# Decode attention with a key/value cache: values summed two key columns per matmul, fewer columns scored on TensorE, short last chunks, a column-shaped output side, and a weight loaded in pieces

## The chip, the cores and the metric

The kernel runs on one core of a Trainium2 chip. The metric is the device time of one execution in microseconds (us). A profile is one further execution under the hardware profiler.

Engine names: PE is TensorE (PEld its weight loads), DVE is VectorE, ACT is ScalarE, SP is the engine that issues the DMAs here. A "DMA engine" is one of the 16 whose busy share the profile's page gives beside these; that is another thing than the engines just named, and most of this study is about one of the 16.

## The reference, cut to what matters

```python
# one query token; H = 32 heads, Sk = 32768 cached keys, Dh = 192, D = 640, Dff = 1536, all bf16
q = (layernorm(x) @ wq).reshape(1, 1, H, Dh).transpose(0, 2, 1, 3)
scores = einsum("bhqd,bhkd->bhqk", q, k_cache) * Dh ** -0.5
o = einsum("bhqk,bhkd->bhqd", softmax(scores), v_cache)
h = x + o.transpose(0, 2, 1, 3).reshape(1, 1, H * Dh) @ wo
out = h + relu(layernorm(h) @ w1) @ w2
```

Each key and value is used once, so the work is reading 805 MB of K and V (2 x 32 x 32768 x 192 x 2 bytes) and about 20 MB of weights.

## The kernel before

A chunk is 4096 keys of one head: 128 partitions with J = 32 key columns of 192 elements each. There are 8 chunks a head, 256 in all. Ten of the 32 columns are scored on TensorE (transpose, copy, matmul), 22 on VectorE, one instruction a column.

```python
J = 32; CH = P * J; NC = Sk // CH; JP = 10; JD = J - JP
kpool = ...tile_pool(name="kpool", bufs=5)          # 5 K tiles, 5 V tiles
vpool = ...tile_pool(name="vpool", bufs=5)

def load_kv(g):                                     # 12288 contiguous bytes a partition
    kt = kpool.tile([P, J * Dh], bf16, name="kt")
    nc.sync.dma_start(out=kt[:], in_=k_hd[h, c * CH:(c + 1) * CH, :].rearrange("(p j) d -> p (j d)", p=P))
    ... # vt the same

def scores_dve(g, mid=None):
    for j in range(JD):
        if j == 4 and mid is not None: mid()        # once a head: the previous head's denominator
        st = scp.tile([P, Dh], bf16, name="st")
        nc.vector.scalar_tensor_tensor(out=st[:], in0=kt[:, j * Dh:(j + 1) * Dh], scalar=1.0, in1=qb[:],
                                       op0=A.mult, op1=A.mult, accum_out=sc[:, j:j + 1])

def pv(g):                                          # o[1, 192] += p_column.T @ V_column, 32 times
    for jj in range(J):
        ...
        nc.tensor.matmul(o[:], lhsT=p, rhs=vt[:, j * Dh:(j + 1) * Dh], start=..., stop=...)

# main loop, cut:
    load_kv(g)
    ... # wo, wq loads
    if c == 0 and h == H // 2:
        nc.sync.dma_start(out=w1_sb[:], in_=B_w1.rearrange("(c p) n -> p c n", p=P))
    if c == 0 and h == H // 2 + 1:
        nc.sync.dma_start(out=w2_sb[:], in_=B_w2.rearrange("(c p) n -> p c n", p=P))
    transposes(g); pv(g - 1); scores_pe(g); scores_dve(g); ...; exp_dve(g, sc)
pv(G - 1); den_mm(H - 1); den_rec(H - 1); o_scale(H - 1); o_turn(...); project(...)
... # layernorm, w1, relu; then the w2 product as rows: 12 x (512 + 128) output columns on one partition
```

The softmax here doesn't subtract the row's maximum and nothing guards it: scores larger than these inputs give would overflow.

Of the kernel before, what the change touches and what calls it, by code (L numbers as in the profile page):

```python
# [13 lines left out]
def kernel(  # L14
# [26 lines left out]
    J = 32  # L41
    CH = P * J
    NC = Sk // CH
    G = H * NC
    JP = 10
    JD = J - JP
    NB = JP * Dh // P
    QG = 4
    assert Sk % CH == 0 and 2 * Dh == 3 * P and JP % 2 == 0 and H % QG == 0 and H % 2 == 0
# [44 lines left out]
    def load_kv(g):  # L94
        h, c = divmod(g, NC)
        kt = kpool.tile([P, J * Dh], bf16, name="kt")
        nc.sync.dma_start(out=kt[:], in_=k_hd[h, c * CH:(c + 1) * CH, :].rearrange("(p j) d -> p (j d)", p=P))
        vt = vpool.tile([P, J * Dh], bf16, name="vt")
        nc.sync.dma_start(out=vt[:], in_=v_hd[h, c * CH:(c + 1) * CH, :].rearrange("(p j) d -> p (j d)", p=P))
        kt_t[g], vt_t[g] = kt, vt  # L100
# [10 lines left out]
    ones_col = const.tile([P, 1], f32)  # L111
# [8 lines left out]
    dsums = const.tile([P, H, 2 * NC], f32)  # L120
    w1_sb = const.tile([P, DT, Dff], bf16)
    w2_sb = const.tile([P, FT, D], bf16)
    o_pair = [const.tile([1, 2 * Dh], f32, name=f"o_pair{i}") for i in range(2)]
# [25 lines left out]
    with tc.manual_schedule():  # L149
# [37 lines left out]
        def transposes(g):  # L187
            kt = kt_t[g]
            kT = tsb.tile([P, NB, P], bf16, name="kT")
            for b0 in range(0, NB, 8):  # L190
                nb = min(8, NB - b0)
                tp = tps.tile([P, 8, P], bf16, name="tp")
                for b in range(nb):
                    off = JD * Dh + (b0 + b) * P
                    nc.tensor.transpose(out=tp[:, b, :], in_=kt[:, off:off + P], identity=ident_b[:])  # L195
                nc.scalar.copy(out=kT[:, b0:b0 + nb, :], in_=tp[:, 0:nb, :])  # L196
            kT_t[g] = kT

        def scores_pe(g):
            kT = kT_t.pop(g)  # L200
            h, c = divmod(g, NC)
            qm = qm_t[h]
            sp = sps.tile([P, JP], f32, name="sp")
            for i in range(JP // 2):
                nc.tensor.matmul(sp[:, 2 * i:2 * i + 2], lhsT=kT[:, 3 * i + 1, :], rhs=qm[:, 1:3],  # L205
                                 start=True, stop=False, skip_group_check=True)
                nc.tensor.matmul(sp[:, 2 * i:2 * i + 1], lhsT=kT[:, 3 * i, :], rhs=qm[:, 0:1],  # L207
                                 start=False, stop=False, skip_group_check=True)
                nc.tensor.matmul(sp[:, 2 * i + 1:2 * i + 2], lhsT=kT[:, 3 * i + 2, :], rhs=qm[:, 3:4],  # L209
                                 start=False, stop=True, skip_group_check=True)  # L210
            pB = pcp.tile([P, JP], bf16, name="pB")
            nc.scalar.activation(out=pB[:], in_=sp[:], func=F.Exp, scale=SCALE,  # L212
                                 accum_out=dsums[:, h, 2 * c + 1:2 * c + 2])
            pB_t[g] = pB

        def scores_dve(g, mid=None):
            kt = kt_t.pop(g)
            h, c = divmod(g, NC)
            qb = qb_t[h]
            sc = scp.tile([P, JD], f32, name="sc")  # L220
            for j in range(JD):
                if j == 4 and mid is not None:
                    mid()
                st = scp.tile([P, Dh], bf16, name="st")
                nc.vector.scalar_tensor_tensor(out=st[:], in0=kt[:, j * Dh:(j + 1) * Dh], scalar=1.0, in1=qb[:],  # L225
                                               op0=A.mult, op1=A.mult, accum_out=sc[:, j:j + 1])
            return sc

        def exp_dve(g, sc):
            h, c = divmod(g, NC)  # L230
            pA = pcp.tile([P, JD], bf16, name="pA")
            nc.scalar.activation(out=pA[:], in_=sc[:], func=F.Exp, scale=SCALE,  # L232
                                 accum_out=dsums[:, h, 2 * c:2 * c + 1])
            pA_t[g] = pA

        def pv(g):
            h, c = divmod(g, NC)
            vt, pA, pB = vt_t.pop(g), pA_t.pop(g), pB_t.pop(g)
            if c == 0:
                o_t[h] = ops.tile([1, Dh], f32, name="o_ps")  # L240
            o = o_t[h]
            for jj in range(J):
                j = jj + JD if jj < JP else jj - JP
                p = pA[:, j:j + 1] if j < JD else pB[:, j - JD:j - JD + 1]
                nc.tensor.matmul(o[:], lhsT=p, rhs=vt[:, j * Dh:(j + 1) * Dh],  # L245
                                 start=(c == 0 and jj == 0), stop=(c == NC - 1 and jj == J - 1))
# [3 lines left out]
        def den_mm(h):  # L250
            d = mm_bank([1, 2 * NC], f32, "den")
# [3 lines left out]
        def den_rec(h):  # L255
            d = den_t.pop(h)
            s = small.tile([1, 2], f32, tag="rec", name="rec")
# [4 lines left out]
        def o_scale(h):  # L262
            s = den_t.pop(h)
            o = o_t.pop(h)
            nc.scalar.activation(out=o_pair[(h // 2) % 2][0:1, (h % 2) * Dh:(h % 2 + 1) * Dh], in_=o[:],  # L265
                                 func=F.Copy, scale=s[0:1, 1:2])
# [3 lines left out]
        def o_turn(pr):  # L270
            ps = mm_bank([P, 3], f32, "oT_ps")
            for b in range(3):
                nc.tensor.transpose(out=ps[:, b:b + 1], in_=o_pair[pr % 2][0:1, b * P:(b + 1) * P],  # L273
                                    identity=ident_f[0:1, 0:1])
# [15 lines left out]
        for g in range(G):  # L290
            h, c = divmod(g, NC)
# [6 lines left out]
            if c == 0 and h == H // 2:  # L298
                nc.sync.dma_start(out=w1_sb[:], in_=B_w1.rearrange("(c p) n -> p c n", p=P))
            if c == 0 and h == H // 2 + 1:  # L300
# [20 lines left out]
        pv(G - 1)  # L321
        den_mm(H - 1)
        den_rec(H - 1)
        o_scale(H - 1)
# [7 lines left out]
        y_a = ops.tile([1, 512], f32, tag="o_ps", name="y_a")  # L332
        y_b = ops.tile([1, P], f32, tag="o_ps", name="y_b")
        for c in range(DT):
            y = y_a[0:1, c * P:(c + 1) * P] if c < 4 else y_b[0:1, :]
            nc.tensor.matmul(y, lhsT=h_col[:, c:c + 1], rhs=ident_f[:], start=(c == 0 or c == 4),  # L336
                             stop=False, skip_group_check=True)
        h1ps = mm_bank([P, FT], f32, "h1ps")
# [6 lines left out]
        for f in range(FT):  # L345
            nc.tensor.matmul(y_a[:], lhsT=h1T[:, f:f + 1], rhs=w2_sb[:, f, 0:512],  # L346
                             start=False, stop=(f == FT - 1), skip_group_check=True)
            nc.tensor.matmul(y_b[:], lhsT=h1T[:, f:f + 1], rhs=w2_sb[:, f, 512:D],  # L348
                             start=False, stop=(f == FT - 1), skip_group_check=True)
        y_row = small.tile([1, D], bf16, tag="y_row", name="y_row")  # L350
        nc.scalar.copy(out=y_row[0:1, 0:512], in_=y_a[:])  # L351
        nc.vector.tensor_copy(out=y_row[0:1, 512:D], in_=y_b[:])
        nc.sync.dma_start(out=out.rearrange("b s d -> (b s) d"), in_=y_row[:])
# [30 lines left out]
```

## Time and profile before

| | before |
|---|---|
| time, median of runs | 2060.8 us (2060.41 to 2061.72) |
| span of the profiled run | 2060.4 us |
| last V tile landed | 2039.3 us |
| from there to the end | 21.1 us |

The first fence is from the page of the kernel before: busy time of each engine; what the 16 DMA engines moved in each of 40 slices of the span; and the DMA queues (packets, MB, share of 16 engines' span). Queue 1 moves 825.00 MB, which is K, V and the weights; the page gives queues 8 and 14 the kind "instruction". Queue 8 is read as TensorE's: its packets (16384 bytes each) are 130 where there are 16643 matmuls, one for every 128 matmuls.

```profile
PE 1405.5 (68%) x16643; PEld 1193.5 (58%) x16643; DVE 1603.1 (78%) x11352; ACT 651.6 (32%) x1719; POOL 0.7 (0%) x6
...
GB/s 395 423 421 420 423 421 423 407 422 420 423 422 357 423 418 423 416 346 425 382 420 344 418 423 421 423 423 393 425 421 422 414 350 423 420 423 417 397 412 77
...
q1 hardware_dynamic: 87596, 825.00, 96.5%
q8 instruction: 130, 2.13, 0.4%
q14 instruction: 118, 0.97, 0.1%
```

The reader sees queue 1 busy for 96.5% of what 16 engines could be, and yet slices at 344 to 393 GB/s among slices at 423. The second fence is the same page's groups for the scoring line (count, then busy us and mean ns of one).

```profile
L225 DVE SCALAR_TENSOR_TENSOR st<-kt,qb 128x192 bf16<-128x192 bf16 x5632 | 1589.7, 350 | 306.7 <-DMA kt<-in_A_k_cache_dram 294.7
...
L225 DVE DVE_READ_ACCUMULATOR st<-kt,qb 128x1 f32 x5632 | 442.4, 79 | 0.1
```

Each column is two rows in the trace on VectorE, the product and the accumulator read. The third fence is from the waits of the kernel before (total us, times, longest).

```profile
DVE st L225 <- DMA kt<-in_A_k_cache_dram: 294.7, 181, 5.7
DVE rec L258 <- PE den L252: 132.8, 32, 5.9
```

VectorE waits for K, so it is not the bound; and once a head it waits about 4 us for the denominator (132.8 us over 32).

**Landings.** The mean DMA share cannot show whether the 16 DMA engines are evenly loaded. The trace has more: a transfer to 128 partitions has 16 semaphore events there. They are read here as one for each of the 16 DMA engines; that is inference from the equal numbers, as no record of the trace names the engine. The following table is worked out from those times (first, ninth, fifteenth and sixteenth landing of a tile in us, then the gap of the sixteenth to that of the tile before).

```
tile    first    ninth  fifteenth  sixteenth   gap
vt      427.4    428.2    430.4      442.2     3.70
kt      431.1    431.9    434.1      446.9     4.66    <- a queue-14 packet started at 444.5
vt      434.8    435.6    437.8      450.6     3.70
kt      438.5    439.3    441.5      454.3     3.70
vt      442.2    443.0    445.2      458.0     3.71
```

Fifteen of the landings come within 3 us; one comes 12 us after them. Over the whole run the sixteenth is 14.8 us behind the fifteenth in the median, 21.3 at most. So one DMA engine is read as running late (that it is always the same one is inferred from the steady cadence), without pausing, and a tile is whole only when it is done. Its gaps are 3.69 us, about what 8 packets of 460 to 464 ns take (an estimate: a tile has 128 packets, 464 ns each in the median, over 16 engines), except for 85 gaps that are about 0.98 us longer. Those end within 5 us after the start of a queue-14 packet of 8192 bytes (85 of the 86 gaps over 4.2 us do), about 130 VectorE instructions after the last of its kind. That is no accident of counting: of all tiles only 23% have such a packet in the 5 us before they land. Such a packet is read as one fetch of VectorE's instructions: 4096 more of them bring 32 more packets below (b_many_small). The 85 gaps add up to 83.5 us. The slow slices are read as the places where the other 15, far ahead, have run out of free buffers: in the one around 650 us their lead falls from 20.6 to 15.0 us, and between 640 and 656 us the issue of a K load waits 5.4 us for VectorE's scoring.

The packet records of the trace show where the 0.98 us goes. Of the 118 packets on queue 14, each 325 ns long in the median, 80 are followed at their end by a K or V packet (12288 bytes) that takes 1.12 us in place of the usual 0.46. The fetch itself and the lengthened packet make 0.325 + 0.66 = 0.98 us.

The last fence of this section is from the timeline at the end of the kernel before (start us, duration us, then engine, line, operation and tiles). It shows the serial tail: the denominator, the residual added by matmuls, w1, the first of the w2 rows, and the store.

```profile
2044.19 0.20 PE L252 MATMUL den<-dsums,ones_col 128*1 128x16 f32 x2
...
2047.49 1.86 PE L336 MATMUL y_a<-ident_f,h_col 128*1 128x128 f32 x8
...
2049.72 1.76 PE L341 MATMUL h1ps<-xn_ln,w_sb 128*128 128x1 bf16 x60
...
2051.75 0.59 PE L346 MATMUL y_a<-w_sb,h1T 128*1 128x512 bf16 x1 [0.27 <-ACT h1T L344]
...
2058.16 0.26 SPq L353 DMA_DIRECT2D out_dram<-y_row  x1
```

### The profile page before, as it was taken

The page shows a single profiled execution, that of the slowest core. Times are in us where ns is not written, and L with a number is a line of the kernel's source. Part 1 is how long each engine was busy: PE and PEld are TensorE (multiplying, and loading weights), DVE is VectorE, ACT ScalarE, POOL GpSimd, SP SyncE. Part 2 cuts the span into 40 slices and gives each one's busy share as a digit, 9 for nine tenths or more (in the row PEclk, how much of TensorE's full clock was granted, in tenths as well). Part 3 has the DMA queues.
Part 4 walks back from the last instruction along what each step waited for, and adds up shares of the span by engine and source line. Part 5 has one row for each costly group of instructions (what it writes and reads, how often), then busy time and mean ns, then how long its engine had stood idle before and what let it go on. Part 6 is the DMA issues. An engine that isn't in the chain of part 4 may idle for free. (4 is left out here: it accounts for less than half of the span.)

```text
span 2060.4 us, 48468 instructions
## 1 busy us (share of the span) xinstructions
PE 1405.5 (68%) x16643; PEld 1193.5 (58%) x16643; DVE 1603.1 (78%) x11352; ACT 651.6 (32%) x1719; POOL 0.7 (0%) x6
## 2 busy tenths in 40 slices
PE   5766666766667666666665666766677667677767
PEld 4555555655555555555555555555566556566555
DVE  6877887778787788777777778887778877788775
ACT  3333333333333233322322333332333323333332
POOL 0000000000000000000000000000000000000000
PEclk9888887788898788888888888898788987878787
DMA  9999999999999999989998999999999989999991
GB/s 395 423 421 420 423 421 423 407 422 420 423 422 357 423 418 423 416 346 425 382 420 344 418 423 421 423 423 393 425 421 422 414 350 423 420 423 417 397 412 77
DMA packets 87844, 828.10 MB, mean 402 GB/s; under 512 B 8619, under 2 KB 21420, under 8 KB 22060
## 3 DMA queue, kind: packets, MB, share of 16 engines
q1 hardware_dynamic: 87596, 825.00, 96.5%
q8 instruction: 130, 2.13, 0.4%
q14 instruction: 118, 0.97, 0.1%
HBM read 824.97 MB, written 0.00 MB: 400 GB/s over the span
## 5 line engine op out<-in xcount | busy, mean ns | idle before, releaser
L225 DVE SCALAR_TENSOR_TENSOR st<-kt,qb 128x192 bf16<-128x192 bf16 x5632 | 1589.7, 350 | 306.7 <-DMA kt<-in_A_k_cache_dram 294.7
L195 PE MATMUL tp<-ident_b,kt 128*128 128x128 bf16 x3840 | 335.3, 255 | 596.6 <-DMA kt<-in_A_k_cache_dram 596.6
L195 PEld LDWEIGHTS <-kt 128*128 128x128 bf16 x3840 | 280.5, 116 | 623.8 <-DMA kt<-in_A_k_cache_dram 623.8
L245 PE MATMUL o_ps<-vt,pA 128*1 128x192 bf16 x5632 | 606.0, 272 | 45.8 <-ACT pA L232 45.6
L245 PEld LDWEIGHTS <-pA 128*1 128x1 bf16 x5632 | 524.9, 95 | 106.4 <-ACT pA L232 55.9
L196 ACT COPY kT<-tp 128x1024 bf16<-128x1024 bf16 (+1 forms) x512 | 465.1, 960 | 347.6 <-PE tp L195 347.3
L225 DVE DVE_READ_ACCUMULATOR st<-kt,qb 128x1 f32 x5632 | 442.4, 79 | 0.1
L245 PE MATMUL o_ps<-vt,pB 128*1 128x192 bf16 x2560 | 354.6, 305 | 0.4 <-ACT pB L212 0.4
L245 PEld LDWEIGHTS <-pB 128*1 128x1 bf16 x2560 | 237.2, 101 | 73.2 <-issue 22.8
L212 ACT ACTIVATE pB<-sp 128x10 bf16<-128x10 f32 x256 | 46.3, 181 | 630.9 <-PE sp L209 627.3
L232 ACT ACTIVATE pA<-sc 128x22 bf16<-128x22 f32 x256 | 56.6, 221 | 397.0 <-DVE st L225 396.8
L205 PEld LDWEIGHTS <-kT 128*128 128x128 bf16 x1280 | 100.0, 96 | 44.2 <-issue 43.3
L205 PE MATMUL sp<-qm,kT 128*128 128x2 bf16 x1280 | 122.3, 166 | 0.4 <-ACT kT L196 0.4
L209 PE MATMUL sp<-qm,kT 128*128 128x1 bf16 x1280 | 118.8, 163 | 0.4 <-ACT kT L196 0.4
L207 PE MATMUL sp<-qm,kT 128*128 128x1 bf16 x1280 | 118.7, 163 | 0.0
L258 DVE TENSOR_REDUCE rec<-den 1x1 f32<-1x16 f32 x32 | 5.2, 162 | 132.8 <-PE den L252 132.8
L207 PEld LDWEIGHTS <-kT 128*128 128x128 bf16 x1280 | 102.6, 96 | 0.0
L209 PEld LDWEIGHTS <-kT 128*128 128x128 bf16 x1280 | 101.4, 95 | 0.5 <-ACT kT L196 0.5
L212 ACT ACTIVATION_READ_ACCUMULATOR pB<-sp 128x1 f32 x256 | 49.9, 195 | 0.1
L232 ACT ACTIVATION_READ_ACCUMULATOR pA<-sc 128x1 f32 x256 | 48.1, 188 | 0.1
L163 PE MATMUL qps<-wq,xn_ln 128*1 128x192 bf16 x160 | 18.7, 248 | 3.3 <-DMA wq<-in_A_wq_dram 3.3
L265 ACT ACTIVATE o_pair<-o_ps,rec 1x192 f32<-1x192 f32 x32 | 13.2, 413 | 8.3 <-DVE rec L259 8.3
(62 smaller groups left out, 145.8 us busy)
## 6 DMA issues: line engine op xcount, KB each, us to landing
kt<-in_A_k_cache_dram SPq DMA_DIRECT2D x256, 1536.0 KB, 30.5
vt<-in_A_v_cache_dram SPq DMA_DIRECT2D x256, 1536.0 KB, 29.0
wq<-in_A_wq_dram SPq DMA_DIRECT2D x8, 960.0 KB, 27.1
wo<-in_A_wo_dram SPq DMA_DIRECT2D x16, 480.0 KB, 28.2
w_sb<-in_B_w_dram SPq DMA_DIRECT2D x2, 1920.0 KB, 32.2
x_row<-in_A_x_dram SPq DMA_DIRECT2D x1, 1.2 KB
out_dram<-y_row SPq DMA_DIRECT2D x1, 1.2 KB
```

The source lines that it names most:

```text
L163: nc.tensor.matmul(qps[:], lhsT=xnT[:, c:c + 1], rhs=wq[:, c, hh * Dh:(hh + 1) * Dh], start=(c == 0), stop=(c == DT - 1))
L195: nc.tensor.transpose(out=tp[:, b, :], in_=kt[:, off:off + P], identity=ident_b[:])
L196: nc.scalar.copy(out=kT[:, b0:b0 + nb, :], in_=tp[:, 0:nb, :])
L205: nc.tensor.matmul(sp[:, 2 * i:2 * i + 2], lhsT=kT[:, 3 * i + 1, :], rhs=qm[:, 1:3], start=True, stop=False, skip_group_check=True)
L207: nc.tensor.matmul(sp[:, 2 * i:2 * i + 1], lhsT=kT[:, 3 * i, :], rhs=qm[:, 0:1], start=False, stop=False, skip_group_check=True)
L209: nc.tensor.matmul(sp[:, 2 * i + 1:2 * i + 2], lhsT=kT[:, 3 * i + 2, :], rhs=qm[:, 3:4], start=False, stop=True, skip_group_check=True)
L212: nc.scalar.activation(out=pB[:], in_=sp[:], func=F.Exp, scale=SCALE, accum_out=dsums[:, h, 2 * c + 1:2 * c + 2])
L225: nc.vector.scalar_tensor_tensor(out=st[:], in0=kt[:, j * Dh:(j + 1) * Dh], scalar=1.0, in1=qb[:], op0=A.mult, op1=A.mult, accum_out=sc[:, ...
L232: nc.scalar.activation(out=pA[:], in_=sc[:], func=F.Exp, scale=SCALE, accum_out=dsums[:, h, 2 * c:2 * c + 1])
L245: nc.tensor.matmul(o[:], lhsT=p, rhs=vt[:, j * Dh:(j + 1) * Dh], start=(c == 0 and jj == 0), stop=(c == NC - 1 and jj == J - 1))
L258: nc.vector.reduce_sum(out=s[:, 0:1], in_=d[:], axis=mybir.AxisListType.X)
L265: nc.scalar.activation(out=o_pair[(h // 2) % 2][0:1, (h % 2) * Dh:(h % 2 + 1) * Dh], in_=o[:], func=F.Copy, scale=s[0:1, 1:2])
```

## The change

Its intent, as the diff reads: halve TensorE's value instructions by giving each matmul two probability columns and two value columns (a 2 x 384 result whose two diagonal blocks are the wanted ones, merged when a head pair is turned into columns); take columns from TensorE and ScalarE (10 to 6) and give them to VectorE; make the last chunks short so that less is left after the last load; produce the output as columns, 60 small matmuls, instead of 24 wide ones on one partition; and load w1 in four column slices, each in 120 and 8 partitions (w2 stays whole and moves to a later head).

```diff
-    JP = 10
+    parts = [(J, 6)] * NC
+    if h == H - 1:
+        parts = [(J, 6)] * (NC - 2) + [(J, 10), (16, 6), (8, 4), (8, 4)]
 ... (load_kv, transposes, scores_pe, scores_dve, exp_dve take jc and jp of their chunk)
-                if j == 4 and mid is not None:
+                if j == 2 and mid is not None:
 ... pv
-            for jj in range(J):
-                nc.tensor.matmul(o[:], lhsT=p, rhs=vt[:, j * Dh:(j + 1) * Dh], ...)
+            for i, j in enumerate(order):               # order: every second column
+                p = pA[:, j:j + 2] if j < JD else pB[:, j - JD:j - JD + 2]
+                nc.tensor.matmul(o[:], lhsT=p, rhs=vt[:, j * Dh:(j + 2) * Dh], ...)
 ... loads
-            if c == 0 and h == H // 2:
-                nc.sync.dma_start(out=w1_sb[:], in_=B_w1.rearrange("(c p) n -> p c n", p=P))
+            if c == 2 and h >= H // 2 and h < H // 2 + 4:
+                ...
+                nc.sync.dma_start(out=w1_sb[0:120, :, i * n1:(i + 1) * n1], in_=w1_view[0:120, :, ...])
+                nc.sync.dma_start(out=w1_sb[120:P, :, i * n1:(i + 1) * n1], in_=w1_view[120:P, :, ...])
 ... end
-        for f in range(FT):
-            nc.tensor.matmul(y_a[:], lhsT=h1T[:, f:f + 1], rhs=w2_sb[:, f, 0:512], ...)
-            nc.tensor.matmul(y_b[:], lhsT=h1T[:, f:f + 1], rhs=w2_sb[:, f, 512:D], ...)
+        for n in range(DT):
+            for f in range(FT):
+                nc.tensor.matmul(yps[:, n:n + 1], lhsT=w2_sb[:, f, n * P:(n + 1) * P], rhs=h1T[:, f:f + 1], ...)
+        nc.vector.tensor_add(out=y_col[:], in0=h_col[:], in1=yps[:])     # then one transpose, one store
```

More of the change, by code (lines that the diff above doesn't have):

```diff
@@ L41 @@
     J = 32
-    CH = P * J
-    NC = Sk // CH
-    G = H * NC
-    JP = 10
-    JD = J - JP
-    NB = JP * Dh // P
-    QG = 4
-    assert Sk % CH == 0 and 2 * Dh == 3 * P and JP % 2 == 0 and H % QG == 0 and H % 2 == 0
+    QG = 4
+    assert Sk % (P * J) == 0 and 2 * Dh == 3 * P and H % QG == 0 and H % 2 == 0
+    NC = Sk // (P * J)
+    chunks = []
+    for h in range(H):
+        parts = [(J, 6)] * NC
+        if h == H - 1:
+            parts = [(J, 6)] * (NC - 2) + [(J, 10), (16, 6), (8, 4), (8, 4)]
+        k0 = 0
+        for c, (jc, jp) in enumerate(parts):
+            chunks.append((h, c, k0, jc, jp))
+            k0 += P * jc
+        assert k0 == Sk
+    G = len(chunks)
+    NCH = [sum(1 for q in chunks if q[0] == h) for h in range(H)]
+    NCM = max(NCH)
+    NBM = max(q[4] for q in chunks) * Dh // P
     const = ctx.enter_context(tc.tile_pool(name="const", bufs=1))
@@ L94, in load_kv @@
     def load_kv(g):
-        h, c = divmod(g, NC)
+        h, c, k0, jc, jp = chunks[g]
         kt = kpool.tile([P, J * Dh], bf16, name="kt")
-        nc.sync.dma_start(out=kt[:], in_=k_hd[h, c * CH:(c + 1) * CH, :].rearrange("(p j) d -> p (j d)", p=P))
+        nc.sync.dma_start(out=kt[:, 0:jc * Dh],
+                          in_=k_hd[h, k0:k0 + P * jc, :].rearrange("(p j) d -> p (j d)", p=P))
         vt = vpool.tile([P, J * Dh], bf16, name="vt")
-        nc.sync.dma_start(out=vt[:], in_=v_hd[h, c * CH:(c + 1) * CH, :].rearrange("(p j) d -> p (j d)", p=P))
+        nc.sync.dma_start(out=vt[:, 0:jc * Dh],
+                          in_=v_hd[h, k0:k0 + P * jc, :].rearrange("(p j) d -> p (j d)", p=P))
         kt_t[g], vt_t[g] = kt, vt
@@ L110 @@
     nc.vector.memset(ones_row[:], 1.0)
-    ones_col = const.tile([P, 1], f32)
+    ones_col = const.tile([P, 2], f32)
     nc.vector.memset(ones_col[:], 1.0)
@@ L119 @@
         nc.vector.memset(r[:], 0.0)
-    dsums = const.tile([P, H, 2 * NC], f32)
+    dsums = const.tile([P, H, 2 * NCM], f32)
+    nc.vector.memset(dsums[:], 0.0)
     w1_sb = const.tile([P, DT, Dff], bf16)
     w2_sb = const.tile([P, FT, D], bf16)
-    o_pair = [const.tile([1, 2 * Dh], f32, name=f"o_pair{i}") for i in range(2)]
+    o_pair = [const.tile([2, 2, 2 * Dh], f32, name=f"o_pair{i}") for i in range(2)]
     attT = aps.tile([P, DT], f32, name="attT")
@@ L188, in transposes @@
             kt = kt_t[g]
-            kT = tsb.tile([P, NB, P], bf16, name="kT")
+            h, c, k0, jc, jp = chunks[g]
+            NB = jp * Dh // P
+            kT = tsb.tile([P, NBM, P], bf16, name="kT")
             for b0 in range(0, NB, 8):
@@ L193, in transposes @@
                 for b in range(nb):
-                    off = JD * Dh + (b0 + b) * P
+                    off = (jc - jp) * Dh + (b0 + b) * P
                     nc.tensor.transpose(out=tp[:, b, :], in_=kt[:, off:off + P], identity=ident_b[:])
@@ L200, in scores_pe @@
             kT = kT_t.pop(g)
-            h, c = divmod(g, NC)
+            h, c, k0, jc, JP = chunks[g]
             qm = qm_t[h]
-            sp = sps.tile([P, JP], f32, name="sp")
+            sp = sps.tile([P, J], f32, name="sp")
             for i in range(JP // 2):
@@ L210, in scores_pe @@
                                  start=False, stop=True, skip_group_check=True)
-            pB = pcp.tile([P, JP], bf16, name="pB")
-            nc.scalar.activation(out=pB[:], in_=sp[:], func=F.Exp, scale=SCALE,
+            pB = pcp.tile([P, J], bf16, name="pB")
+            nc.scalar.activation(out=pB[:, 0:JP], in_=sp[:, 0:JP], func=F.Exp, scale=SCALE,
                                  accum_out=dsums[:, h, 2 * c + 1:2 * c + 2])
@@ L217, in scores_dve @@
             kt = kt_t.pop(g)
-            h, c = divmod(g, NC)
+            h, c, k0, jc, jp = chunks[g]
+            JD = jc - jp
             qb = qb_t[h]
-            sc = scp.tile([P, JD], f32, name="sc")
+            sc = scp.tile([P, J], f32, name="sc")
             for j in range(JD):
-                if j == 4 and mid is not None:
+                if j == 2 and mid is not None:
                     mid()
@@ L229, in exp_dve @@
         def exp_dve(g, sc):
-            h, c = divmod(g, NC)
-            pA = pcp.tile([P, JD], bf16, name="pA")
-            nc.scalar.activation(out=pA[:], in_=sc[:], func=F.Exp, scale=SCALE,
+            h, c, k0, jc, jp = chunks[g]
+            JD = jc - jp
+            pA = pcp.tile([P, J], bf16, name="pA")
+            nc.scalar.activation(out=pA[:, 0:JD], in_=sc[:, 0:JD], func=F.Exp, scale=SCALE,
                                  accum_out=dsums[:, h, 2 * c:2 * c + 1])
@@ L236, in pv @@
         def pv(g):
-            h, c = divmod(g, NC)
+            h, c, k0, jc, jp = chunks[g]
+            JD = jc - jp
             vt, pA, pB = vt_t.pop(g), pA_t.pop(g), pB_t.pop(g)
             if c == 0:
-                o_t[h] = ops.tile([1, Dh], f32, name="o_ps")
+                o_t[h] = ops.tile([2, 2 * Dh], f32, name="o_ps")
             o = o_t[h]
-            for jj in range(J):
-                j = jj + JD if jj < JP else jj - JP
-                p = pA[:, j:j + 1] if j < JD else pB[:, j - JD:j - JD + 1]
-                nc.tensor.matmul(o[:], lhsT=p, rhs=vt[:, j * Dh:(j + 1) * Dh],
-                                 start=(c == 0 and jj == 0), stop=(c == NC - 1 and jj == J - 1))
+            order = list(range(JD, jc, 2)) + list(range(0, JD, 2))
+            for i, j in enumerate(order):
+                p = pA[:, j:j + 2] if j < JD else pB[:, j - JD:j - JD + 2]
+                nc.tensor.matmul(o[:], lhsT=p, rhs=vt[:, j * Dh:(j + 2) * Dh],
+                                 start=(c == 0 and i == 0), stop=(c == NCH[h] - 1 and i == len(order) - 1))
         den_t = {}
         def den_mm(h):
-            d = mm_bank([1, 2 * NC], f32, "den")
+            d = mm_bank([2, 2 * NCM], f32, "den")
             nc.tensor.matmul(d[:], lhsT=ones_col[:], rhs=dsums[:, h, :], start=True, stop=True)
@@ L256, in den_rec @@
             d = den_t.pop(h)
-            s = small.tile([1, 2], f32, tag="rec", name="rec")
+            s = small.tile([2, 2], f32, tag="rec", name="rec")
             nc.vector.reduce_sum(out=s[:, 0:1], in_=d[:], axis=mybir.AxisListType.X)
@@ L260, in den_rec, with o_scale @@
             den_t[h] = s
-        def o_scale(h):
+        def o_scale(h, last=False):
             s = den_t.pop(h)
             o = o_t.pop(h)
-            nc.scalar.activation(out=o_pair[(h // 2) % 2][0:1, (h % 2) * Dh:(h % 2 + 1) * Dh], in_=o[:],
-                                 func=F.Copy, scale=s[0:1, 1:2])
+            dst = o_pair[(h // 2) % 2]
+            n0 = (h % 2) * Dh
+            nc.scalar.activation(out=dst[:, 0, n0:n0 + Dh], in_=o[:, 0:Dh], func=F.Copy, scale=s[:, 1:2])
+            if last:
+                nc.vector.tensor_scalar_mul(out=dst[:, 1, n0:n0 + Dh], in0=o[:, Dh:2 * Dh], scalar1=s[:, 1:2])
+            else:
+                nc.scalar.activation(out=dst[:, 1, n0:n0 + Dh], in_=o[:, Dh:2 * Dh], func=F.Copy, scale=s[:, 1:2])
         oT_t = {}
         def o_turn(pr):
+            src = o_pair[pr % 2]
             ps = mm_bank([P, 3], f32, "oT_ps")
             for b in range(3):
-                nc.tensor.transpose(out=ps[:, b:b + 1], in_=o_pair[pr % 2][0:1, b * P:(b + 1) * P],
-                                    identity=ident_f[0:1, 0:1])
+                for i in range(2):
+                    nc.tensor.matmul(ps[:, b:b + 1], lhsT=src[:, i, b * P:(b + 1) * P], rhs=ident_f[0:2, i:i + 1],
+                                     start=(i == 0), stop=(i == 1))
             oT = small.tile([P, 3], bf16, tag="oT", name="oT")
@@ L290 @@
         for g in range(G):
-            h, c = divmod(g, NC)
+            h, c, k0, jc, jp = chunks[g]
             if g > 0:
@@ L297 @@
                 load_wq(h // QG + 1)
-            if c == 0 and h == H // 2:
-                nc.sync.dma_start(out=w1_sb[:], in_=B_w1.rearrange("(c p) n -> p c n", p=P))
-            if c == 0 and h == H // 2 + 1:
+            if c == 2 and h >= H // 2 and h < H // 2 + 4:
+                i = h - H // 2
+                n1 = Dff // 4
+                w1_view = B_w1.rearrange("(c p) n -> p c n", p=P)
+                nc.sync.dma_start(out=w1_sb[0:120, :, i * n1:(i + 1) * n1], in_=w1_view[0:120, :, i * n1:(i + 1) * n1])
+                nc.sync.dma_start(out=w1_sb[120:P, :, i * n1:(i + 1) * n1], in_=w1_view[120:P, :, i * n1:(i + 1) * n1])
+            if c == 2 and h == H // 2 + 4:
                 nc.sync.dma_start(out=w2_sb[:], in_=B_w2.rearrange("(c p) n -> p c n", p=P))
@@ L320 @@
             exp_dve(g, sc)
-        pv(G - 1)
         den_mm(H - 1)
         den_rec(H - 1)
-        o_scale(H - 1)
+        pv(G - 1)
+        o_scale(H - 1, last=True)
         o_turn(H // 2 - 1)
@@ L331 @@
         hnT = layernorm_col(h_col, "ln2")
-        y_a = ops.tile([1, 512], f32, tag="o_ps", name="y_a")
-        y_b = ops.tile([1, P], f32, tag="o_ps", name="y_b")
-        for c in range(DT):
-            y = y_a[0:1, c * P:(c + 1) * P] if c < 4 else y_b[0:1, :]
-            nc.tensor.matmul(y, lhsT=h_col[:, c:c + 1], rhs=ident_f[:], start=(c == 0 or c == 4),
-                             stop=False, skip_group_check=True)
-        h1ps = mm_bank([P, FT], f32, "h1ps")
+        h1ps = ops.tile([P, FT], f32, tag="o_ps", name="h1ps")
         for f in range(FT):
@@ L344 @@
         nc.scalar.activation(out=h1T[:], in_=h1ps[:], func=F.Relu)
-        for f in range(FT):
-            nc.tensor.matmul(y_a[:], lhsT=h1T[:, f:f + 1], rhs=w2_sb[:, f, 0:512],
-                             start=False, stop=(f == FT - 1), skip_group_check=True)
-            nc.tensor.matmul(y_b[:], lhsT=h1T[:, f:f + 1], rhs=w2_sb[:, f, 512:D],
-                             start=False, stop=(f == FT - 1), skip_group_check=True)
-        y_row = small.tile([1, D], bf16, tag="y_row", name="y_row")
-        nc.scalar.copy(out=y_row[0:1, 0:512], in_=y_a[:])
-        nc.vector.tensor_copy(out=y_row[0:1, 512:D], in_=y_b[:])
-        nc.sync.dma_start(out=out.rearrange("b s d -> (b s) d"), in_=y_row[:])
+        yps = ops.tile([P, DT], f32, tag="o_ps", name="yps")
+        for n in range(DT):
+            for f in range(FT):
+                nc.tensor.matmul(yps[:, n:n + 1], lhsT=w2_sb[:, f, n * P:(n + 1) * P], rhs=h1T[:, f:f + 1],
+                                 start=(f == 0), stop=(f == FT - 1))
+        y_col = small.tile([P, DT], f32, tag="y_col", name="y_col")
+        nc.vector.tensor_add(out=y_col[:], in0=h_col[:], in1=yps[:])
+        ytp = mm_bank([DT, P], f32, "ytp")
+        nc.tensor.transpose(out=ytp[:], in_=y_col[:], identity=ident_f[:])
+        y_row = small.tile([DT, P], bf16, tag="y_row", name="y_row")
+        nc.vector.tensor_copy(out=y_row[:], in_=ytp[:])
+        nc.sync.dma_start(out=out.rearrange("b s (c p) -> (b s c) p", p=P), in_=y_row[:])
 _INS = ['A_x', 'A_k_cache', 'A_v_cache', 'A_wq', 'A_wo', 'B_x', 'B_w1', 'B_w2']
```

## The prediction

> **What bounds the kernel now.** The page gives DMA queue 1 96.5% of 16 engines' span; TensorE is 68% busy, VectorE 78%. The queue is not evenly loaded. Each transfer raises its semaphore 16 times; in the trace's landing times the sixteenth of a K or V tile comes 3.69 us after that of the tile before, throughout, while the fifteenth is up to 20 us earlier. One DMA engine is late and sets the pace; the slices at 344 to 393 GB/s are the others waiting for buffers. Gaps of 4.67 us instead of 3.69 follow within 5 us of an 8 KB instruction-fetch packet on queue 14 that comes each time VectorE has issued some 130 instructions. So a VectorE fetch costs that engine 0.98 us; 11614 instructions are 91 fetches, 89 us. Sum for that engine (estimate): 512 tiles x 3.69 + 52 for weights (their packet durations) + 89 + start = 2032 us; the last tile landed at 2039. TensorE's 130 fetches (queue 8) do not show in these gaps.[...]
>
> After the last V landing a serial tail of 21.1 us follows (the timeline).
>
> **The change.**
> - TensorE: 32 value matmuls of 192 columns become 16 of 384[...], transposes 15 to 9 a chunk. Not critical: gain 0; fetches fall to about 75, at most -2 us.
> - ScalarE: one kT copy of 0.9 us less per chunk. Not critical.
> - VectorE: 22 to 26 columns a chunk at 0.279 us: 6.1 to 7.25 us, against 7.9 us of supply. The stall for the denominator once a head (132.8 us over 32 in the waits, 4.15 each) stays near 4. Per head 58 + 0.3 + 4 = 62.4 us against 64: just behind the DMA.
> - VectorE instructions: 11614 to about 13640, 16 more fetches x 0.98 = **+15.5 us** on the late engine, critical.
> - w1 in pieces of 120 and 8 partitions: [...]
> - Tail: last chunk of 8 columns instead of 32, second FFN product as 60 column matmuls (the first took 1.76 us for 60) instead of 5.8 us of row matmuls, 2.2 us of residual matmuls gone: 21.1 to about 12.5, **-8.6 us**.
>
> Sum: 2060.8 + 15.5 - 4.8 - 8.6 - 2 = about **2061 us**. Range 2048 to 2074. Chances: faster by over 2% 0.05, within 2% 0.90, slower by over 2% 0.05.
>
> **What would show it.** Right: queue 14 packets up by about 16; the last tile landing at 2047 to 2051, its sixteenth still over 15 us late; VectorE near 91%; tail 12 to 13 us. Wrong: last landing near 2000 (TensorE's fetches were the load), or VectorE 96% busy without waits for K (it is the bound).
>
> **What would make it wrong.** VectorE has only 2% of slack: a denominator stall of 6 us would make it the bound, towards 2080. If fewer TensorE fetches relieve the late engine, about 2020. If it is not spared w1, add 5.

A term of the sum: 4.8 us off for w1 in pieces, the 40 packets of 121 ns that w1 in one transfer is estimated to put on the late engine, on the assumption that this engine is spared the pieces. The assumption was not shown by any trace. The sum of about 2061 us still contains the term; without it, it comes to 2060.8 + 15.5 - 8.6 - 2 = 2065.7 us. The 2 us for TensorE's fetches were an allowance that no run had given.

## The result, and the profile after

The changed kernel takes 2085.8 us (median of 4; 2084.21 to 2087.49), the kernel before 2061.0 beside it. The ratio is 1.012, 95% interval 1.0103 to 1.0138: slower, by less than 2%. A ratio is the mean time of one kernel's runs over that of the other's of the same rounds, so not quite the ratio of the medians.

| | before | after |
|---|---|---|
| span of the profiled run | 2060.4 | 2085.7 |
| last V tile landed | 2039.3 | 2069.7 |
| from there to the end | 21.1 | 16.0 |
| sixteenth landing behind the fifteenth, median | 14.8 | 15.3 |
| VectorE instructions (all rows of its queue) | 11614 | 13643 |

The loads end 30.4 us later, the tail is 5.1 us shorter; 30.4 - 5.1 = 25.3 us is the whole difference of the two profiles. The page of the changed kernel, the same lines:

```profile
PE 1363.5 (65%) x9682; PEld 680.4 (33%) x9682; DVE 1877.1 (90%) x13379; ACT 493.8 (24%) x1759; POOL 0.7 (0%) x6
...
GB/s 395 424 421 421 423 422 424 379 422 422 417 396 355 424 413 420 393 360 424 350 406 382 359 394 413 344 423 419 424 422 424 406 369 424 414 416 382 412 396 130
...
q1 hardware_dynamic: 90176, 825.00, 96.2%
q8 instruction: 75, 1.23, 0.2%
q14 instruction: 135, 1.11, 0.1%
```

TensorE's weight loads went from 58% to 33% and its fetches (queue 8) from 130 to 75, as meant; the run a_jp10_w1_one below shows that nothing came of it. Queue 14 has 17 packets more. The groups:

```profile
L242 DVE SCALAR_TENSOR_TENSOR st<-kt,qb 128x192 bf16<-128x192 bf16 x6644 | 1863.4, 344 | 57.7 <-DMA kt<-in_A_k_cache_dram 55.1
...
L242 DVE DVE_READ_ACCUMULATOR st<-kt,qb 128x1 f32 x6644 | 487.0, 73 | 0.0
```

VectorE has 6644 columns instead of 5632. In the waits it still waits for K, though 55 us instead of 295:

```profile
DVE rec L278 <- PE den L272: 137.6, 32, 6.1
...
DVE st L242 <- DMA kt<-in_A_k_cache_dram: 55.1, 44, 5.7
```

So VectorE is close to being the bound, but the late DMA engine is still read as the bound: its gaps in this trace are again 3.69 us, 101 of them about 0.98 longer (99.3 us together). What is new stands around the w1 pieces. The landings of the second slice, as before (the piece of 8 partitions raises its semaphore 9 times):

```
tile       first    last but one     last     gap of the last
kt        1086.0      1087.9        1100.6    4.67   <- a fetch at 1096.9
vt        1089.7      1091.6        1104.3    3.70
kt        1093.4      1095.3        1110.2    5.89   <- no fetch near it
vt        1097.1      1099.0        1113.9    3.66
kt        1100.8      1102.7        1117.6    3.68
vt        1104.6      1108.9        1122.2    4.64
w1, 120   1092.8      1110.0        1124.8    2.61
w1, 8     1104.2      1109.4        1125.0    0.18
```

Both w1 pieces have one landing 15 us after the others, so the late engine is read as taking part in both: it is not spared. The eight pieces cost it 10.1 us with their own gaps, where w1 in one transfer took it 4.8 (an estimate: 640 packets over 16 engines are 40, of 121 ns; its own gap was 5.83 us with a VectorE fetch of 0.98 in it). And each slice has one K or V tile with a longer gap (here 5.89), at the time when the other engines, 15 us ahead, move the slice: 1.9, 2.2, 1.8 and 3.0 us too much in the four slices (a VectorE fetch falls into the last). The issues of the pieces, from the DMA view of the changed kernel (count, KB each, median us from issue to landing where known):

```profile
w_sb<-in_B_w_dram SPq DMA_DIRECT2D x4, 450.0 KB, 30.2
...
w_sb<-in_B_w_dram SPq DMA_DIRECT2D x4, 30.0 KB
```

The tail of the changed kernel, from the chain that ended last (start us, duration us, what):

```profile
2069.09 1.46 PE o_ps L265 x8
2070.55 0.11 PE sp L221
...
2071.24 0.81 ACT kT L212
...
2072.99 0.21 PE den L272 x2
...
2078.92 1.75 PE h1ps L366 x60
...
2080.92 1.75 PE yps L373 x60
```

The w2 product now takes 1.75 us in place of 5.8, and the w1 product starts right after the layernorm. But 3.3 us pass between the last V landing at 2069.7 and the denominator at 2072.99: the three short chunks still have to go through TensorE and ScalarE one after the other (value matmuls of one, scores and copy of the next). The store, from the timeline:

```profile
2083.64 0.31 SPq L381 DMA_DIRECT2D out_dram<-y_row  x1
```

### The profile page after: what moved, and what is told of

It reads as the page before. It is cut to its first block, busy times and chain, and to the rows that moved or that the text cites. A ratio compares the mean times of both kernels' runs of the same rounds, so it can differ in the third digit from the quotient of the medians. Undisturbed runs are those within 1.5% of the kernel's fastest.

```text
span 2085.7 us, 36636 instructions
## 1 busy us (share of the span) xinstructions
PE 1363.5 (65%) x9682; PEld 680.4 (33%) x9682; DVE 1877.1 (90%) x13379; ACT 493.8 (24%) x1759; POOL 0.7 (0%) x6
## 5 line engine op out<-in xcount | busy, mean ns | idle before, releaser
L242 DVE SCALAR_TENSOR_TENSOR st<-kt,qb 128x192 bf16<-128x192 bf16 x6644 | 1863.4, 344 | 57.7 <-DMA kt<-in_A_k_cache_dram 55.1
L265 PE MATMUL o_ps<-vt,pA 128*2 128x384 bf16 x3322 | 828.0, 418 | 230.9 <-ACT pA L250 230.3
L265 PEld LDWEIGHTS <-pA 128*2 128x2 bf16 x3322 | 334.0, 104 | 717.2 <-issue 303.5
L211 PE MATMUL tp<-ident_b,kt 128*128 128x128 bf16 x2322 | 217.8, 253 | 477.8 <-DMA kt<-in_A_k_cache_dram 477.3
L211 PEld LDWEIGHTS <-kt 128*128 128x128 bf16 x2322 | 165.1, 113 | 500.9 <-DMA kt<-in_A_k_cache_dram 499.7
L212 ACT COPY kT<-tp 128x1024 bf16<-128x1024 bf16 (+2 forms) x514 | 301.1, 636 | 97.4 <-PE tp L211 96.9
L250 ACT ACTIVATE pA<-sc 128x26 bf16<-128x26 f32 (+1 forms) x258 | 58.0, 225 | 715.3 <-DVE st L242 715.3
L265 PE MATMUL o_ps<-vt,pB 128*2 128x384 bf16 x774 | 216.0, 398 | 0.1
L221 PEld LDWEIGHTS <-kT 128*128 128x128 bf16 x774 | 62.8, 97 | 103.1 <-issue 101.4
L223 PE MATMUL sp<-qm,kT 128*128 128x1 bf16 x774 | 81.2, 163 | 0.0
L225 PE MATMUL sp<-qm,kT 128*128 128x1 bf16 x774 | 81.2, 163 | 0.0
L223 PEld LDWEIGHTS <-kT 128*128 128x128 bf16 x774 | 65.4, 98 | 0.0
L225 PEld LDWEIGHTS <-kT 128*128 128x128 bf16 x774 | 64.0, 96 | 0.0
```

The costliest lines, as they stand in the source:

```text
L211: nc.tensor.transpose(out=tp[:, b, :], in_=kt[:, off:off + P], identity=ident_b[:])
L212: nc.scalar.copy(out=kT[:, b0:b0 + nb, :], in_=tp[:, 0:nb, :])
L221: nc.tensor.matmul(sp[:, 2 * i:2 * i + 2], lhsT=kT[:, 3 * i + 1, :], rhs=qm[:, 1:3], start=True, stop=False, skip_group_check=True)
L223: nc.tensor.matmul(sp[:, 2 * i:2 * i + 1], lhsT=kT[:, 3 * i, :], rhs=qm[:, 0:1], start=False, stop=False, skip_group_check=True)
L225: nc.tensor.matmul(sp[:, 2 * i + 1:2 * i + 2], lhsT=kT[:, 3 * i + 2, :], rhs=qm[:, 3:4], start=False, stop=True, skip_group_check=True)
L250: nc.scalar.activation(out=pA[:, 0:JD], in_=sc[:, 0:JD], func=F.Exp, scale=SCALE, accum_out=dsums[:, h, 2 * c:2 * c + 1])
```

## The experiments

Two theories. Theory 1: the late DMA engine bounds the kernel, and its time is its share of the bytes plus 0.98 us for each VectorE fetch plus what w1 costs it. Theory 2, the rival: VectorE has become too slow (7.25 us a chunk and a stall a head), K buffers come free late, and that is what slows the loads. All twelve kernels gave correct results; each was run with three rounds beside the kernel before. First the account of the landings in each profile:

```
kernel            VectorE rows  queue-14 packets  last V landed   tail    span
before               11614            118             2039.3      21.1   2060.4
b_one_long           11870            120             2043.4      23.0   2066.4
b_jp6                13662            134             2057.4      24.4   2081.8
b_many_small         15710            150             2070.4      20.1   2090.5
b_w1_split           11614            118             2052.5      19.5   2072.0
b_lean                1084             33             1975.1      21.7   1996.8
after                13643            135             2069.7      16.0   2085.7
a_w1_one             13643            135             2059.1      15.9   2075.0
a_w1_cols            13643            135             2059.9      16.2   2076.1
a_w1_96_32           13643            135             2065.9      15.9   2081.8
a_w1_parts           13643            135             2070.4      16.0   2086.4
a_jp10_w1_one        11611            119             2040.5      15.0   2055.5
a_lean                1095             35             1970.4      15.4   1985.9
a_lean_half           1384             37             1970.4      14.7   1985.1
```

(b_ is built on the kernel before, a_ on the changed one.) From the kernel before to the one with 16 small instructions a chunk: 32 more packets, the last landing 31.1 us later, 0.97 us a packet. Each row is one profiled run, and the runs of one kernel differ by 1 to 5 us, so a difference of 1 or 2 us between two rows means nothing.

### VectorE instructions without much VectorE time, and the reverse

```diff
 b_many_small: in the loop over the 22 columns
+                if j >= JD - 16:
+                    nc.vector.memset(pad_s[:, j - JD + 16:j - JD + 17], 0.0)      # 16 a chunk, one element
 b_one_long: in the same loop
+                if j == JD - 1:
+                    nc.vector.memset(pad_s[:], 0.0)                                # 1 a chunk, 960 elements
```

> The kernel before with 16 one-element VectorE memsets added to each chunk: 4096 more instructions, 32 more instruction fetches, and about 1 us more VectorE time a chunk (6.1 to about 7.1, against 7.9 of supply). Theory 1 (each VectorE fetch costs the late DMA engine 0.98 us): +31 us, about 2092, last tile landing near 2071, queue 14 packets up by about 32. Theory 2 (VectorE's time a chunk, and so when K buffers come free, is what counts): the same time as the run with one long memset.

> The kernel before with one VectorE memset of 960 fp32 elements added to each chunk: 256 more instructions, 2 more fetches, but again about 1 us more VectorE time a chunk. Theory 1: +2 us, about 2063. Theory 2: as slow as the run with 16 small memsets, +20 to +30.

Measured: 2091.13 us with the small ones, ratio 1.0145 (1.0129 to 1.0160); 2065.61 us with the long one, ratio 1.0017 (1.0000 to 1.0034). From the page of the kernel with 16 small memsets a chunk (busy time and instructions; queue 14):

```profile
PE 1391.3 (67%) x16643; PEld 1186.7 (57%) x16643; DVE 1636.6 (78%) x15448; ACT 651.8 (31%) x1719; POOL 0.7 (0%) x6
...
q14 instruction: 150, 1.23, 0.1%
```

And of the kernel with one long memset a chunk:

```profile
PE 1404.3 (68%) x16643; PEld 1187.8 (57%) x16643; DVE 1806.8 (87%) x11608; ACT 647.8 (31%) x1719; POOL 0.7 (0%) x6
...
q14 instruction: 120, 0.98, 0.1%
```

The long memsets (0.80 us each by the busy times, 1806.8 - 1603.1 over 256) make VectorE busier (87%) than the small ones (78%), and it is the kernel with the small ones that is slow. It has 30 packets more on queue 14 and lands 27.0 us later. One part of the expectation missed: 16 small memsets cost VectorE only 33 us over the run and not about 256; in the timeline each (59 ns) lies within the span of the next column's product. That makes the separation cleaner: VectorE waits for K as long as before (296.8 us, 294.7 before). Theory 1 holds with its number, though the long memsets land 4.1 us later where their two fetches make 2; theory 2 falls for this kernel.

### Only the columns moved

```diff
 b_jp6
-    JP = 10
+    JP = 6
```

> The kernel before with one number changed: 6 columns of 32 on TensorE instead of 10, so 26 on VectorE. Theory 1: VectorE instructions +2048, 16 fetches, +15.7 us, about 2076.5, with TensorE's own fetches hardly changed. Theory 2 (VectorE became the bound): VectorE would wait for K nowhere, and the time would be 32 heads of 62.5 us and more, 2030 to 2060 plus the tail. If TensorE's load mattered instead, faster than before.

Measured: 2081.78 us, ratio 1.0097 (1.0082 to 1.0112). The last landing is 18.1 us later, with 102 long gaps (100.8 us) in place of 85. The rest of the 20 us is its tail: 24.4 us, probably as the last chunk now has 26 columns on VectorE. (The profiled run was the slowest of its four, 1.8 us over their median.) Its page:

```profile
PE 1342.9 (65%) x13571; PEld 1075.4 (52%) x13571; DVE 1880.1 (90%) x13400; ACT 484.0 (23%) x1719; POOL 0.7 (0%) x6
...
q14 instruction: 134, 1.10, 0.1%
```

TensorE had fewer instructions (106 packets on queue 8) and that gained nothing. VectorE is at 90%, as in the changed kernel. Moving four columns to VectorE is by itself most of the change's loss.

### The rest of the change, without the columns and without the w1 pieces

```diff
 a_jp10_w1_one: on the changed kernel
-        parts = [(J, 6)] * NC
+        parts = [(J, 10)] * NC          # the last four chunks stay 32, 16, 8, 8
 ... and the w1 and w2 loads as in the kernel before
```

> The changed kernel with 10 columns on TensorE again and w1 and w2 loaded whole as before: what is left of the change is values in column pairs, short last chunks and the column output side. Theory 1: only the tail (-5 us) and nothing for the halved TensorE fetches: about 2056. If TensorE's fetches (130 to about 90) relieve the late engine, some 20 us less, about 2036.

Measured: 2056.81 us, ratio 0.9978 (0.9963 to 0.9992). The last landing is where it was before (2040.5); the tail is 15.0 us. Queues 8 and 14 of its page:

```profile
PE 1430.5 (70%) x12730; PEld 829.8 (40%) x12730; DVE 1601.9 (78%) x11347; ACT 660.7 (32%) x1759; POOL 0.7 (0%) x6
...
q8 instruction: 99, 1.62, 0.3%
q14 instruction: 119, 0.97, 0.1%
```

TensorE's fetches fell from 130 to 99 and the last landing did not move. Value pairs were worth nothing here, where the late engine bounds the kernel, and the short chunks and the column output were worth their tail (21.1 to 15.0 us).

### The w1 load

```diff
 a_w1_one: on the changed kernel, w1 and w2 whole, at the old places
+            if c == 0 and h == H // 2:
+                nc.sync.dma_start(out=w1_sb[:], in_=B_w1.rearrange("(c p) n -> p c n", p=P))
 a_w1_cols: the four column slices, each over 128 partitions in one transfer
+                nc.sync.dma_start(out=w1_sb[:, :, i * n1:(i + 1) * n1], in_=w1_view[:, :, i * n1:(i + 1) * n1])
 a_w1_parts: once, full width, in 120 and 8 partitions
+                nc.sync.dma_start(out=w1_sb[0:120, :, :], in_=w1_view[0:120, :, :])
+                nc.sync.dma_start(out=w1_sb[120:P, :, :], in_=w1_view[120:P, :, :])
 a_w1_96_32: the four slices, each in 96 and 32 partitions
 b_w1_split: the kernel before with the changed kernel's w1 and w2 loads
```

> The changed kernel with w1 and w2 loaded whole in one transfer each, at the old place. In the changed kernel's trace both w1 pieces (120 and 8 partitions) have one landing 10 to 20 us after the others, so the late engine takes part in both. Theory 1: the pieces cost the late engine 20 us (10 for the pieces themselves, 10 for longer gaps of the tiles just before them), the whole load 5: about 15 us less than the changed kernel, 2071. Theory 2 (VectorE is the bound of the changed kernel): no change, 2085.

Measured: 2076.84 us, ratio 1.0068 (1.0053 to 1.0083): 9 us faster than the changed kernel by the medians, 10.7 by the ratios to the kernel before (the two ran in different sessions), not 15. The last landing is 10.6 us earlier. The expectation was too large: it had booked every excess in the w1 stretch on w1, and two of VectorE's fetches fall there, which explains about 2 us of the 4.

> The changed kernel with w1 in the same four column slices but each over all 128 partitions in one transfer. If the 768-byte rows cost: the late engine's share is 4 x 2.6 = 10.4 us instead of 4.8, about 2076 to 2077. If it is the 8-partition piece (its issue held the queue 7 to 11 us) that costs the longer gaps, those are gone here; if slicing costs them, 2085 stays.

Measured: 2076.68 us, ratio 1.0069 (1.0054 to 1.0084). The slices cost the late engine 5.6 us in all, hardly more than w1 in one transfer, and no tile near them has a longer gap without a fetch. So neither slicing nor the shorter rows cost anything that counts here.

> The changed kernel with w1 loaded once, full width, in 120 and 8 partitions. Rows of 3072 bytes as before. If the 8-partition piece costs a longer gap each time, once instead of four times: about 5 + 2.5 us on the late engine, 2073. Its issue should again take about 10 us instead of 0.3. If only slicing costs, 2071.

Measured: 2087.63 us, ratio 1.0124 (1.0109 to 1.0139), where 2073 had been expected. One split in partitions is as bad as four: the piece of 120 has a gap of 9.7 us on the late engine where w1 loaded whole has 5.8 (a VectorE fetch falls into each), and a V and a K tile before it have 3.9 (again with a fetch) and 3.6 us too much, at the time when the other engines move the piece. So the same bytes in split form cost the same in one pair of pieces as in four. The idea in the expectation that a long issue of the 8-partition piece is the cause also fell: issues of 8 to 22 us follow the whole loads of w1 and w2 too (9.4 us for the K tile after w1 loaded whole), and cost the late engine nothing, probably as it has some 30 us of work queued (a K tile lands 29.0 us after its issue in the changed kernel, in the median).

> The kernel before with the changed kernel's w1 pieces and its places of the w1 and w2 loads, nothing else. Theory 1: +15 us, about 2076. If the pieces cost only where VectorE is short of time, +0 to +6.

Measured: 2076.55 us, ratio 1.0069 (1.0052 to 1.0086). The last landing is 13.2 us later. The cost is there with VectorE at 77%, so it isn't one of the changed kernel's VectorE.

> The changed kernel with its w1 slices split at partition 96 instead of 120. [...]If any split of the partitions that no longer sits like the 128-partition tiles costs, the late engine again loses some 4 to 5 us a slice: about 2085.

Measured: 2083.01 us, ratio 1.0101 (1.0086 to 1.0116). Both pieces have 16 landings and yet the last landing is 6 us later than with unsplit slices: own gaps 9.1 us in place of 5.6, and again tiles with 1.2 to 1.3 us too much beside them (2.3 where a fetch falls in). So a piece need not have fewer landings than 16 to cost. That it is enough to divide the partitions in another way than for the 128-partition tiles fits all four split runs, but no run shows it by itself.

The packet records show what is slow: not more bytes and not the issue, but each packet. K and V packets that start while the bulk of a w1 load moves (10 to 60 of them a load or slice) take 464 to 471 ns in the median where w1 isn't split (a_w1_one, a_w1_cols), as everywhere else. They take 893 in a_w1_parts, 696 to 929 in the slices of the changed kernel, 714 to 756 in b_w1_split and 549 to 766 in a_w1_96_32. w1's own packets of 768 bytes take 58 ns in the changed kernel and 36 in a_w1_cols.

### VectorE instructions taken away

```diff
 a_lean: on a_jp10_w1_one (b_lean: the same on the kernel before)
-            for j in range(JD):
-                st = scp.tile([P, Dh], bf16, name="st")
-                nc.vector.scalar_tensor_tensor(out=st[:], in0=kt[:, j * Dh:(j + 1) * Dh], ..., accum_out=sc[:, j:j + 1])
+            st = prp.tile([P, 22, Dh], bf16, name="st")
+            nc.vector.tensor_tensor(out=st[:, 0:JD, :], in0=kt[:, 0:JD * Dh].rearrange("p (j d) -> p j d", d=Dh),
+                                    in1=qb[:].unsqueeze(1).to_broadcast([P, JD, Dh]), op=A.mult)
+            nc.vector.reduce_sum(out=sc[:, 0:JD], in_=st[:, 0:JD, :], axis=mybir.AxisListType.X)
 a_lean_half: before the sum, the upper half of each row is added to the lower; the sum then runs over 96
+            nc.vector.tensor_tensor(out=st[:, 0:JD, 0:Dh // 2], in0=st[:, 0:JD, 0:Dh // 2],
+                                    in1=st[:, 0:JD, Dh // 2:Dh], op=A.add)
```

> The kernel before with VectorE's 22 product-and-sum instructions a chunk (44 in the trace, with their accumulator reads) replaced by one product over all 22 columns and one sum over the inner axis. VectorE instructions fall from 11614 to about 900, 91 fetches to about 7. Theory 1: if VectorE keeps up, the late engine loses 82 us of work: last tile near 1957 to 1965, 1980 to 1990 in all, and the sixteenth landing only a few us late. [...]Theory 2 (fetches do not matter): about 2060 as long as VectorE takes under 7.9 us a chunk.

Measured: 1999.79 us, ratio 0.9700 (0.9686 to 0.9715). The last landing is 64.2 us earlier. From its page:

```profile
PE 1383.8 (69%) x16643; PEld 1170.5 (59%) x16643; DVE 1779.6 (89%) x600; ACT 647.4 (32%) x1719; POOL 0.7 (0%) x6
...
q14 instruction: 33, 0.27, 0.0%
...
L227 DVE TENSOR_REDUCE sc<-st 128x22 f32<-128x4224 bf16 x256 | 1164.5, 4549 | 23.1
...
L223 DVE TENSOR_TENSOR st<-kt,qb 128x4224 bf16<-128x4224 bf16 x256 | 603.6, 2358 | 86.0 <-DMA kt<-in_A_k_cache_dram 71.8
```

This is the plainest test: nothing but VectorE's instructions was changed, VectorE is busier than before (89% and 78%), and the kernel is 3% faster.

> The same replacement in the changed kernel with 10 columns on TensorE and w1 loaded whole. Theory 1: as the run on the kernel before, less 5 us of tail: 1970 to 1985. If VectorE is the bound: as that run.

Measured: 1988.19 us, ratio 0.9643 (0.9627 to 0.9659): the fastest with the next, 3.6% faster than the kernel before, of which 0.2% were there without the larger instructions (a_jp10_w1_one). From its page: busy times, GB/s in 40 slices, queues, and the two VectorE groups:

```profile
PE 1395.4 (70%) x12730; PEld 796.6 (40%) x12730; DVE 1780.3 (90%) x607; ACT 656.4 (33%) x1759; POOL 0.7 (0%) x6
...
GB/s 396 424 422 421 425 421 425 422 421 424 422 424 421 422 425 422 424 419 424 422 423 399 421 423 423 422 424 421 423 423 423 424 419 425 423 424 423 423 424 223
...
q1 hardware_dynamic: 88180, 825.00, 99.3%
...
q14 instruction: 35, 0.29, 0.0%
...
L244 DVE TENSOR_REDUCE sc<-st 128x22 f32<-128x4224 bf16 (+1 forms) x258 | 1164.0, 4512 | 24.4 <-DVE st L240 1.5
...
L240 DVE TENSOR_TENSOR st<-kt,qb 128x4224 bf16<-128x4224 bf16 (+1 forms) x258 | 603.6, 2340 | 71.7 <-DMA kt<-in_A_k_cache_dram 58.8
```

VectorE is 90% busy, as in the changed kernel, and the kernel is 98 us faster: that busy share was not what bound it. Queue 14 has 35 packets, the slow slices are gone, and the sixteenth landing is 0.1 us behind the fifteenth in the median, 1.5 at most. In b_lean the product of 4224 elements a partition took 2358 ns (1.8 elements a ns), the sum 4549 ns (0.93 a ns); why the product is about twice as fast was not shown. In the code the product is stored in a bf16 tile before it is summed; the result still agreed with the reference.

The expectation of 1957 to 1965 for the last landing was 10 us too low for b_lean, or more. With the late engine relieved, another term shows: every eighth TensorE fetch is followed by a gap 1.5 us too long on the engine that now lands last (every 121 us, with a fetch every 15). In a_lean, with 99 fetches in place of 130, that is every 160 us and 1.2 us each, and the last landing is 4.7 us earlier. So fewer TensorE instructions seem to be worth something after VectorE's fetches are gone; a_lean has the rest of the change too, so it isn't shown by itself.

> As the run before this one, with a third instruction that first adds the upper half of each product row to the lower in bf16, so that the sum runs over 96 elements. About 256 instructions more (2 fetches). [...]Theory 1: if VectorE was the bound of the run before, it no longer is, 1970 to 1980; else the same time.

Measured: 1988.00 us, ratio 0.9641 (0.9627 to 0.9655). VectorE falls to 78% busy and the time stays, so VectorE was not the bound of a_lean either. What bounds both is read as the DMA with all engines alike: queue 1 is at 99.3% in a_lean and 99.4% here.

## Why the prediction was right or wrong

**Right: what bounds the kernel.** One DMA engine is late, as the landings are read, and VectorE's fetches make it late, 0.98 us each (the sixteenth landing was 14.8 us behind before, 0.1 us in a_lean). Adding instructions (b_many_small, 31.1 us later for 32 packets), moving columns (b_jp6, 18.1 us later for 17 more long gaps) and taking instructions away (b_lean, 64.2 us earlier) all moved the last landing in the direction that says, the first two by about its amount. Of the signs that the prediction named, the packets of queue 14 (+17), the lateness of the sixteenth landing (15.3 us) and VectorE (90%) came; the last landing (2069.7, not 2047 to 2051) and the tail (16.0 us, not 12 to 13) did not.

**Right in mechanism, a little small: the fetches.** Predicted "+15.5 us" for 16 more; the kernel with the columns alone has 17 more long gaps and lands 18.1 us later, in a profiled run 1.8 us slower than its median.

**Wrong: the w1 term.** The sum took 4.8 us off for w1 in pieces, as if the late engine took no part in them. No run had shown that, and the prediction booked the favourable case. In the traces the 120-partition piece raises its semaphore 16 times and the 8-partition piece 9 times, and the last of each comes 12 to 19 us after the one before, so the late engine is read as taking part in both. The measured term is **+10.6 us** (last landing of the changed kernel against w1 loaded whole), 15 us off, and this is most of the miss. "If it is not spared w1, add 5" saw the first half of it; that a piece also costs the late engine twice its own time and slows the tiles in flight was not seen.

**Half right: the tail.** Predicted 21.1 to 12.5 us, "-8.6"; measured 16.0, -5.1. The two timelines show which terms were off:

- The w2 product, up to the store: 6.4 to 2.7 us, 3.7 saved of the 4.0 booked.
- The residual matmuls: 0.8 saved of the 2.2 booked. In the kernel before they ran (2047.5 to 2049.8) while the layernorm did its steps on VectorE and ScalarE (2047.6 to 2048.9), and those steps remain.
- Between the denominator and the residual column h_col: 2.2 to 3.4 us, a cost of 1.2 that was not booked. The last value matmuls, a second scaling and twice the turning matmuls now stand there.
- From the last landing to the denominator: 4.9 to 3.3 us, 1.6 saved where the rest of the sum, 2.4, was booked. The three short chunks pass through TensorE and ScalarE one after the other.

**Right: TensorE's gain of 0; wrong: the -2 us that the sum took for its fetches ("at most -2 us").** They do not show on the late engine: 130 to 99 packets moved the last landing by +1.2 us in a_jp10_w1_one, which is nothing.

**Not tested: VectorE's slack.** The warning that VectorE might become the bound did not come true: K waits of 55 us remained and nearly every long gap has its fetch or its w1 slice (of the 101, 99 have a fetch in the 5 us before). How near it came is not measured.

The sum as measured, from the profiles: +18.1 for the columns, +1.7 for what else lies between b_jp6 and a_w1_one, +10.6 for the w1 pieces, -5.1 for the tail: 25.3 us. The single terms are as sure as single profiles are, to 1 or 2 us.

**Open.** Why the packets slow down while a load split by partitions moves, so that it costs the late engine twice its own time (10.1 against 4.8 us) and slows tiles beside it. Unsplit slices cost nothing (2076.68 us, 2076.84 with w1 whole) and every split did; no run shows the reason. Nor is it shown which DMA engine is the late one, or why the packet that follows a fetch takes 1.12 us.

## What to carry to other kernels

When a kernel is bound by DMA, look at the spread of a transfer's sixteen landings before looking at the mean: one late engine cost 3% or more here, at a mean busy share of 96.5%. Here the fetches of 11614 small VectorE instructions cost that engine 83.5 us; fewer, larger instructions alone paid 3.0% (b_lean), with VectorE busier than before (89% and 78%). And w1 cut by partitions moved the last landing 10.6 us back, where it was meant to spare the late engine 4.8 us.
